# A third PSUM bank in both score tiles of a planned attention kernel, lent to side work when it is free

## The chip, the cores and the metric

One core of a Trainium2 chip. The metric is the device time of one execution in microseconds (us). TensorE is PE in the profile (PEld: its weight loads), VectorE is DVE, ScalarE is ACT, GpSimd is POOL. The profiled span runs from the first to the last instruction; it is 1.8 to 2.0 us shorter than the device time of the same execution. The profiled execution need not be the median one: the old kernel's has a span of 925.2 us, the median is 929.9 us.

## The reference

Two attention blocks over the same tokens (2048 tokens, width 640, 32 heads of 20), mixed by a gate per token:

```python
g = sigmoid((x * gate_w).sum(-1, keepdims=True))
a = softmax_attention(x, A_wqkv) @ A_wo        # full 2048 x 2048 scores, 32 heads
b = dilated_window_attention(x, B_wqkv) @ B_wo # 8 keys at distance 0, 2, ..., 14
return g * a + (1 - g) * b
```

Block A costs 2048 "units", each a 128 x 512 piece of scores that must be made by TensorE, passed through an exponential, and multiplied with V (PV). A head group is 64 units (four heads, 512 queries); there are 32.

## The kernel before

The Python program *plans*: it keeps an estimated clock per engine, lets generators (projections, block B, output) ask for TensorE time, VectorE time or a PSUM bank, and appends each instruction to its engine's list when the estimate says that it fits. The hardware then runs those lists with semaphores. So a small edit can move thousands of instructions.

Main loop, in short: take two or three units, make their scores (`qk`), take their exp on ScalarE, run PV of tiles two or more back, fill the rest of TensorE's time with side work (projections, block B, output), then with throw-away "filler" matmuls (`filler`). Some units skip ScalarE: each is a "ride", which VectorE copies out of PSUM; four rides make a "quad", from which VectorE makes five "slices" of exponentials.

```python
TSZ = (3, 2)                                   # banks of the two score tiles
score = [ps(512 * TSZ[0], "score0"), ps(512 * TSZ[1], "score1")]
obank = ps(512, "obank")                       # PV result
side = [ps(512, "side0"), ps(512, "side1")]    # for all other matmuls
NE = 6                                         # exp buffers, 1536 or 1024 wide
ebuf = [sb([P, 512 * TSZ[i % 2]], BF16, "ebuf%d" % i) for i in range(NE)]
NS = 3                                         # buffers of exp slices made by VectorE
...
def qk(s):                                     # scores of tile s; [cut]
    t = T("pe", 0.215, fn, reads=..., writes=[("score", s % 2)], mode="row")
    if rides[s]:                               # a "ride": unit 3 goes to VectorE, not ScalarE
        run_dve(t.end + LAT["pe"] - 0.35)
        T("dve", 0.69, lambda e: e.tensor_scalar(uD[...], o, UOFF, 0.0, op0=ALU.add, op1=ALU.max),
          reads=[("score", s % 2)], writes=[("uD", d % 2, i)])
def exp(s):
    n = len(tiles[s])
    exps[s] = T("act", actc(512 * n), lambda e: e.activation(
        ebuf[s % NE][:, 0:512 * n], score[s % 2][:, 0:512 * n], ACTF.Exp, scale=LN2 / STEP), ...)
...
def gen_d(d):                                  # five slices per ridden quad: int16 bit tricks for exp
    T("dve", 0.11 + 0.1334 * n, lambda e: e.tensor_scalar(eD[:, sl % NS, 0:512 * n].bitcast(I16),
      uD[d % 2][:, 0:512 * n], 0.25, SHIFTS[k], op0=ALU.mult, op1=ALU.add), ...)
def gen_bweights():                            # rearranges block B's weights, once
    for m in range(3):
        for c in range(CN):
            T("pool", 2.2, lambda e, o=o, i=i: e.tensor_copy(o, i), ...)   # 15 copies, 128 x 640
...
while pvg < NG:                                # main loop
        while s >= NE and pvq and tile_of[pvq[0]][0] <= s - NE:
            hold = 0                           # exp buffer of tile s not yet free:
            _, last = pv_slot(s, True)         # PV is forced, before the scores of tile s
            ...
        us = next_tile()
        ...
        qk(s); exp(s)
        if s >= hold and (s % 2 == 0 or ...):
            got, last = pv_slot(...)           # the regular place of PV
        spend(exps[s - 1].end + SLACK[len(us) - 2])   # side work and filler
```

Of the kernel before, what the change touches and what calls it, by code (L numbers as in the profile page):

```python
# [14 lines left out]
P = 128  # L15
# [3 lines left out]
DH = 20  # L19
# [226 lines left out]
def _build(ctx, nc, A_x, A_wqkv, A_wo, B_wqkv, B_wo, gate_w, out):  # L246
# [6 lines left out]

    TSZ = (3, 2)
    score = [ps(512 * TSZ[0], "score0"), ps(512 * TSZ[1], "score1")]
    obank = ps(512, "obank")
    side = [ps(512, "side0"), ps(512, "side1")]


    NE = 6  # L260
    NV0 = 2
# [7 lines left out]
    qT = [sb([P, 512], BF16, "qT%d" % i) for i in range(2)]  # L269
    ebuf = [sb([P, 512 * TSZ[i % 2]], BF16, "ebuf%d" % i) for i in range(NE)]  # L270
    NSLOT = 16
# [150 lines left out]

    bank_free = [0.0, 0.0]
    bank_used = [False, False]

# [6 lines left out]
    def release(b, t):  # L432
        bank_used[b] = False
        bank_free[b] = t.end + LAT[t.stream]

# [81 lines left out]
    def gen_v(half):  # L517
        for kb in range(NV0 if half == 0 else 0, KBN):
            b = yield from bank()
            mms = [(side[b][:, 0:320], xT[:, c, kb * P:(kb + 1) * P],  # L520
                    kvw[:, WV_OFF + c * D + half * 320:WV_OFF + c * D + half * 320 + 320]) for c in range(CN)]
            yield from mm_group(b, mms, ["WvA"] + XT(kb // 4), mmc(320))
            yield ("dve",)
            o = _ap(vA, (kb * NQ + 4 * half) * 4 * DV + 1, [[DV, 16], [1, DH]])
            i = _ap(side[b], 0, [[DH, 16], [1, DH]])
            t = T("dve", dvc(320), lambda e, o=o, i=i: e.tensor_copy(o, i), reads=[("side", b), "vAones"],
                  writes=[("vA", kb, half)])
            release(b, t)
            done[("v", kb, half)] = True
# [81 lines left out]
    def gen_bproj(u):  # L611
# [4 lines left out]
        for m in range(3):  # L616
# [5 lines left out]
            for f0 in range(0, CN, 2):  # L622
# [10 lines left out]
                o = tt[:, f0:f0 + n, off:off + TOK]  # L633
                i = _ap(side[b], 0, [[TOK, n], [1, TOK]])
                t = TB(dvc(n * TOK), lambda e, o=o, i=i: e.tensor_copy(o, i), reads=[("side", b)], writes=[key])
# [5 lines left out]
    def gen_b(u):  # L641
# [28 lines left out]
        if u == 0:  # L670
            yield ("pe", 0.06, 0.0)
            ob = _ap(side[b], 0, [[TOK, 2], [1, 16]])
            T("pe", 0.06, lambda e, ob=ob: e.matmul(ob, ident[:, :], maskB[:, :, :], start=False, stop=True, skip_group_check=True),
              reads=["ident", "maskB"], accum=[("side", b)])
# [57 lines left out]
        for f0 in range(0, CN, 2):  # L732
# [6 lines left out]
            o = oB[:, f0:f0 + n, hu * TOK:(hu + 1) * TOK]  # L739
            i0 = _ap(side[b], 0, [[TOK, n], [1, TOK]])  # L740
            i1 = _ap(rB, 0, [[0, n], [1, TOK]])
# [118 lines left out]
    def step(ent, limit, force):  # L860
# [10 lines left out]
        elif req[0] == "act":  # L871
            if not force and req[1] > sch.avail["act"]:
                return False
        elif req[0] == "bank":
            best = None
            for b in range(2):
                if not bank_used[b] and (best is None or bank_free[b] < bank_free[best]):
                    best = b
            if best is None or (not force and bank_free[best] > now):
                return False  # L880
            bank_used[best] = True
            send = best
        try:
# [6 lines left out]
        return moved  # L890

    def run_side(limit, force=False):
        while True:
            for ent in list(gens):
                if ent in gens and step(ent, limit, force):
# [22 lines left out]
    def turn(tcc, c0, c1, s_):  # L918
# [10 lines left out]

        T("pe", 0.065 * 4 * (c1 - c0), fn, reads=[("xs", tcc), "ident"], writes=[("score", s_)])  # L930

# [5 lines left out]
    def x_out(tcc):  # L937
        cols = slice(tcc * 512, (tcc + 1) * 512)
        T("act", actc(1536), lambda e: e.activation(  # L939
            xT[:, 0:3, cols], _ap(score[0], 0, [[512, 3], [1, 512]]), ACTF.Copy), reads=[("score", 0)], writes=[("xT", tcc, 0)])  # L940
        T("dve", dvc(1024), lambda e: e.tensor_copy(xT[:, 3:5, cols], _ap(score[1], 0, [[512, 2], [1, 512]])),
# [48 lines left out]
    for i in range(4):  # L990
# [9 lines left out]
    k_out(0)  # L1000
    T("pe", 1.07, proj5(side[1][:, :], lambda c: WqP[:, c, :], None, 0), reads=WQ + XT(0), writes=[("side", 1)])
    k_first(1)
# [6 lines left out]
    T("dve", dvc(512), lambda e: e.tensor_scalar(  # L1009
        qabs[:, :].bitcast(U16), side[1][:, :].bitcast(U16)[:, 1:1024:2], 0x7FFF, None, op0=ALU.bitwise_and),  # L1010
      reads=[("side", 1)], writes=["qabs"])
    k_max(2)
# [7 lines left out]
      reads=[("kmx", 0), "KMmask"], writes=[("KM", 0)])  # L1020
    T("pe", 0.215, lambda e: e.matmul(side[1][:, :], KM[0][:, :], qabs[:, :], start=False, stop=True, skip_group_check=True),
      reads=[("KM", 0), "qabs"], accum=[("side", 1)])
    t = k_out(3)
    obank_first = t.end + LAT["act"]
    v_out(0, 2, 1)
    t = T("dve", dvc(512), lambda e: e.tensor_scalar(qT[0][:, :], side[1][:, :], OCT, offs[:, 0:1], op0=ALU.mult, op1=ALU.add),
          reads=[("side", 1), "offs"], writes=[("qT", 0)])
    bank_free[0] = bank_free[1] = t.end + LAT["dve"]
    done[("k", 0)] = done[("q", 0)] = True
# [37 lines left out]

    DWAIT = 0.6

    def wanted(js):  # L1070
# [72 lines left out]
    def next_tile():  # L1143
        s = len(tiles)
        n = TSZ[s % 2]
        us = []
        ride = None
        while len(us) < n and cur["g"] < NG:
# [8 lines left out]
            if lo == 4 * hi:  # L1157
                cur["g"] += 1
                continue
            if n == 3 and len(us) == 2 and not ride:  # L1160
                ride = wanted([j for j in range(4) if all(uu % 4 != j for uu in us)])
# [9 lines left out]
        return us  # L1171

    def qk(s):
        us = tiles[s]
        sc = score[s % 2]
        lst = [(uu // 64, uu % 64 // 4, uu % 4, sc[:, i * 512:(i + 1) * 512]) for i, uu in enumerate(us)]
        if rides[s]:
            d, i, j = rides[s]
            o = sc[:, 1024:1536]
            lst.append((*dquads[d], j, o))  # L1180

# [9 lines left out]
        for g, kb, j, _ in lst:  # L1191
            rd.add(("kT", GROUPS[g][1], kb // 4))
            rd.add(("qT", g % 2))
        t = T("pe", 0.215, fn, reads=sorted(rd, key=str), writes=[("score", s % 2)], mode="row")
        if rides[s]:

            run_dve(t.end + LAT["pe"] - 0.35)
            T("dve", 0.69, lambda e: e.tensor_scalar(  # L1198
                uD[d % 2][:, 512 * i:512 * (i + 1)], o, UOFF, 0.0, op0=ALU.add, op1=ALU.max),
              reads=[("score", s % 2)], writes=[("uD", d % 2, i)])  # L1200
            if d == len(dquads) - 1 and not dopen:
                d_close()

    def exp(s):
        n = len(tiles[s])
        exps[s] = T("act", actc(512 * n), lambda e: e.activation(  # L1206
            ebuf[s % NE][:, 0:512 * n], score[s % 2][:, 0:512 * n], ACTF.Exp, scale=LN2 / STEP),
          reads=[("score", s % 2)], writes=[("ebuf", s % NE)])

# [36 lines left out]
    def filler(limit):  # L1246

        if sch.load(2.3) >= FILL:
            return False
        best = [b for b in range(2) if not bank_used[b] and bank_free[b] <= sch.avail["pe"]]  # L1250
        if best:
# [93 lines left out]
    while pvg < NG:  # L1345
# [44 lines left out]
        if acting:  # L1390
            lim = (exps[s - 1].end if s >= 1 else sch.avail["act"]) + SLACK[len(us) - 2]
            spend(lim)
# [36 lines left out]
```

## Time and profile before

929.9 us (median; one run took 1967 us and is left out).

Groups of instructions with different shapes kept apart (count, then busy us and mean ns, then the engine's idle time before them): the two widths of exp, and the two groups of filler.

```profile
L1206 ACT ACTIVATE ebuf<-score 128x1024 bf16<-128x1024 f32 x585 | 578.3, 1033 | 11.5 <-PE score L1186 8.5
L1206 ACT ACTIVATE ebuf<-score 128x1536 bf16<-128x1536 f32 x234 | 342.6, 1464 | 1.4 <-PE score L1186 0.7 <-ACT ebuf L1206 0.2
L1260 PE MATMUL obank<-xT,zero 128*32 128x512 bf16 x1240 | 100.4, 382 | 0.0
L1260 PE MATMUL side<-xT,ident 128*32 128x512 bf16 x452 | 37.2, 382 | 0.0
```

Durations overlap: neighbouring exps start 0.904 us (narrow) or 1.331 us (wide) apart when nothing delays them. I call 585 x 0.904 + 234 x 1.331 = 840.3 us the *floor* of the exps, and what start-to-start times exceed it by their *lateness*. (An exp's own duration is 1.03 us, so one that waits for its scores already loses 0.13 us before the profile shows idle time.) The span is then: 21.0 us head, 840.3 floor, 47.3 lateness, 16.4 tail (0.1 us is the last exp's own overlap).

The tail, as the timeline of ScalarE shows it (start, duration; in brackets idle time and who ended it):

```profile
907.27 1.45 ACT L1206 ACTIVATE ebuf<-score 128x1536 bf16<-128x1536 f32 x1
920.65 1.08 ACT L811 ACTIVATE stage<-side 128x512 bf16<-128x512 f32 x2 [11.93 <-PE side L792]
```

After the last exp TensorE still has 11 us of output projection to do.

### The profile page before, as it was taken

What the parts mean: (1) busy time and instruction counts of PE and PEld (TensorE: products, weight loads), DVE (VectorE), ACT (ScalarE), POOL (GpSimd) and SP (SyncE); (2) the same over time, 40 slices, a digit from 0 to 9 for tenths busy, and PEclk for the clock granted to TensorE, in tenths of its full rate; (3) what the DMA queues carried; (4) which work ended last, traced back from release to release, by engine and by line L of the source; (5) the groups of instructions that cost most, each with busy time, mean ns of one, the idle gap of its engine ahead of it and who ended that gap; (6) DMA issues with size and microseconds to landing.
All of it is one profiled execution on the core that took longest, in us unless ns stands there. A gap on an engine that the chain in (4) does not pass through costs nothing.

```text
span 925.2 us, 31488 instructions
## 1 busy us (share of the span) xinstructions
PE 908.8 (98%) x13998; PEld 322.6 (35%) x13998; DVE 676.6 (73%) x1173; ACT 889.1 (96%) x854; POOL 25.5 (3%) x23
## 2 busy tenths in 40 slices
PE   8999999998999999999999999999999999999997
PEld 4433332222333333333433343343343333433333
DVE  6667767887778768866886687577775956886862
ACT  6999999998999999999999999999999999999993
POOL 1000000008000000000000000000000000000000
PEclk9999999999999999999999999999999999999999
DMA  6121000030000010001100100110000001100000
GB/s 194 27 54 10 7 2 6 6 113 7 6 7 2 7 21 7 7 2 14 14 7 7 21 7 2 14 14 7 6 7 16 7 6 15 14 7 1 3 2 30
DMA packets 89027, 16.27 MB, mean 18 GB/s; under 512 B 81596, under 2 KB 88252, under 8 KB 88892
## 3 DMA queue, kind: packets, MB, share of 16 engines
q1 hardware_dynamic: 88892, 14.27, 9.5%
q8 instruction: 110, 1.80, 0.8%
q14 instruction: 25, 0.20, 0.1%
HBM read 11.63 MB, written 2.62 MB: 15 GB/s over the span
## 4 chain that ended last, share of the span: by engine, by line
PE 77%; ACT 18%; issue 3%; DVE 1%; DMA 0%; DVEq 0%; ACTq 0%
PE side L449 26%; PE score L1186 24%; ACT ebuf L1206 18%; PE obank L1239 16%; PE obank L1260 6%; PE side L1260 2%; PE side L662 1%; PE side L717 1%; DMA oTn<-in_A_x_dram 0%; PE score L926 0%; DVE eD L587 0%; ACT xT L939 0%; PE obank L947 0%; PE side L947 0%; DVE oTt L570 0%
## 5 line engine op out<-in xcount | busy, mean ns | idle before, releaser
L1206 ACT ACTIVATE ebuf<-score 128x1024 bf16<-128x1024 f32 (+1 forms) x819 | 871.4, 1156 | 13.0 <-PE score L1186 9.3
L1186 PE MATMUL score<-qT,kT 32*128 32x512 bf16 x2048 | 334.6, 384 | 7.2 <-ACT ebuf L1206 3.4
L1198 DVE TENSOR_SCALAR uD<-score 128x512 uint16<-128x512 f32 x176 | 121.1, 688 | 107.1 <-PE score L1186 105.0
L1186 PEld LDWEIGHTS score<-qT,kT 32*128 32x128 bf16 x2048 | 79.8, 91 | 284.4 <-issue 131.5
L1239 PE MATMUL obank<-ebuf,vA 128*21 128x512 bf16 x1872 | 175.3, 385 | 2.0 <-DVE eD L587 1.4
L587 DVE TENSOR_SCALAR eD<-uD 128x2048 int16<-128x2048 uint16 x220 | 146.0, 692 | 9.9 <-PE obank L1239 8.9
L449 PE MATMUL side<-xT,kvw 128*32 128x256 bf16 (+1 forms) x2960 | 141.1, 294 | 0.0
L1260 PE MATMUL obank<-xT,zero 128*32 128x512 bf16 x1240 | 100.4, 382 | 0.0
L449 PEld LDWEIGHTS side<-xT,kvw 128*32 128x32 bf16 x2960 | 69.4, 96 | 45.5 <-issue 22.4
L1239 PEld LDWEIGHTS obank<-ebuf,vA 128*21 128x21 bf16 x1872 | 41.3, 89 | 110.6 <-issue 93.1
L1239 PE MATMUL obank<-eD,vA 128*21 128x512 bf16 x880 | 71.2, 379 | 0.0
L729 DVE TENSOR_TENSOR stage<-vB,repB 128x1280 bf16<-128x1280 bf16 x64 | 50.4, 820 | 0.9
L449 PE MATMUL side<-stage,ident 128*32 128x512 bf16 (+1 forms) x768 | 50.2, 346 | 0.0
L652 DVE TENSOR_TENSOR stage<-qB,kB 128x1280 bf16<-128x1280 bf16 x64 | 49.7, 817 | 0.1
L449 PE MATMUL side<-woA_r,oTn 128*32 128x512 bf16 (+1 forms) x992 | 49.3, 300 | 0.0
L449 PE MATMUL side<-xT,WqP 128*32 128x512 bf16 x620 | 48.4, 382 | 0.0
L1260 PEld LDWEIGHTS obank<-xT,zero 128*32 128x32 bf16 x1240 | 28.3, 95 | 33.6 <-issue 21.7
L1260 PE MATMUL side<-xT,ident 128*32 128x512 bf16 x452 | 37.2, 382 | 0.0
L449 PE MATMUL side<-woBp,oB 128*32 128x512 bf16 (+1 forms) x640 | 33.7, 301 | 0.5 <-issue 0.5
L449 PE MATMUL side<-kvw,xT 128*32 128x320 bf16 x600 | 30.6, 300 | 0.2 <-DVE qT L512 0.2
L472 DVE TENSOR_SCALAR kT<-side,onesrow 128x512 bf16<-128x512 f32 x28 | 21.0, 749 | 12.3 <-PE side L449 12.2
L742 DVE SCALAR_TENSOR_TENSOR oB<-side,rB 128x512 bf16<-128x512 f32 (+1 forms) x24 | 14.4, 598 | 19.8 <-PE side L449 19.7
(122 smaller groups left out, 575.5 us busy)
## 6 DMA issues: line engine op xcount, KB each, us to landing
WqP<-in_A_wqkv_dram SPq DMA_DIRECT2D x150, 20.0 KB, 2.3
stage<-in_B_wqkv_dram SPq DMA_DIRECT2D x1, 2400.0 KB, 9.1
out_dram<-outsb SPq DMA_DIRECT2D x12, 160.0 KB, 1.9
oTn<-in_A_x_dram SPq DMA_DIRECT2D x2, 640.0 KB, 5.2
kvw<-in_A_wqkv_dram SPq DMA_DIRECT2D x1, 800.0 KB, 8.8
stage<-in_A_wqkv_dram SPq DMA_DIRECT2D x1, 800.0 KB, 9.9
woA_r<-in_A_wo_dram SPq DMA_DIRECT2D x4, 200.0 KB
woBp<-in_B_wo_dram SPq DMA_DIRECT2D x5, 160.0 KB
```

What stands on the lines that cost most here:

```text
L449: ins = e.matmul(o[32 * j:32 * j + 32, :], l[:, 32 * j:32 * j + 32], r, start=(first and i == 0), stop=(last and i == n - 1), skip_group_c ...
L472: t = T("dve", dvc(512), lambda e, b=b, tcc=tcc: e.tensor_scalar(kT[:, q, tcc * 512:(tcc + 1) * 512], side[b][:, :], onesrow[:, 0:1], None ...
L587: T("dve", 0.11 + 0.1334 * n, lambda e, k=k, sl=sl: e.tensor_scalar(eD[:, sl % NS, 0:512 * n].bitcast(I16), uD[d % 2][:, 0:512 * n], 0.25, ...
L652: TB(dvc(CN * TOK, 2), lambda e, w=w, ks=ks: e.tensor_tensor(prodB(w), qB[:, :, :], ks, ALU.mult), reads=["qB", "kB"], writes=[("prod", w) ...
L662: ins = e.matmul(side[b][32 * w4:32 * w4 + 32, half * TOK:(half + 1) * TOK], Sel, pr, start=(half == 0 and f == 0), stop=(half == 1 and f ...
L729: TB(dvc(CN * TOK, 2), lambda e, w=w, vs=vs, rr=rr: e.tensor_tensor(prodB(w), vs, rr, ALU.mult), reads=["vB", ("repB", w4 % 2)], writes=[( ...
L742: t = TB(dvc(n * TOK), lambda e, o=o, i0=i0, i1=i1: e.scalar_tensor_tensor(o, i0, -0.5, i1, op0=ALU.mult, op1=ALU.mult), reads=[("side", b ...
L1186: ins = e.matmul(o, kT[32 * j:32 * j + 32, q, kb * P:(kb + 1) * P], qT[g % 2][32 * j:32 * j + 32, :], start=True, stop=True)
L1198: T("dve", 0.69, lambda e: e.tensor_scalar(uD[d % 2][:, 512 * i:512 * (i + 1)], o, UOFF, 0.0, op0=ALU.add, op1=ALU.max), reads=[("score", ...
L1206: exps[s] = T("act", actc(512 * n), lambda e: e.activation(ebuf[s % NE][:, 0:512 * n], score[s % 2][:, 0:512 * n], ACTF.Exp, scale=LN2 / S ...
L1239: ins = e.matmul(obank[32 * j:32 * j + DV, :], vA[:, kb, GROUPS[g][1], j, :], src, start=(kb == 0), stop=(last and k >= len(lst) - 4), ski ...
L1260: ins = e.matmul(o[32 * j:32 * j + 32, :], w[:, 32 * j:32 * j + 32], xT[:, 0, 0:512], start=bool(best), stop=bool(best), skip_group_check= ...
```

## The change

Both score tiles get three banks. The third bank of each is a shared resource: for a wide exp, for a ride to VectorE, or for side work. One side bank stays fixed. At most two of the three are held by side work at once. To fit, the exp buffers become five of 1536 (the same bytes as six alternating ones).

```diff
-    TSZ = (3, 2)
-    score = [ps(512 * TSZ[0], "score0"), ps(512 * TSZ[1], "score1")]
+    score = [ps(1536, "score0"), ps(1536, "score1")]
-    side = [ps(512, "side0"), ps(512, "side1")]
-    NE = 6
+    sbank = ps(512, "side0")
+    BANKS = [(sbank, 0), (score[0], 1024), (score[1], 1024)]
+    side = [t_[:, o_:o_ + 512] for t_, o_ in BANKS]
+    NE = 5
-    ebuf = [sb([P, 512 * TSZ[i % 2]], BF16, "ebuf%d" % i) for i in range(NE)]
+    ebuf = [sb([P, 1536], BF16, "ebuf%d" % i) for i in range(NE)]
@@ bank request: a lent bank only if no matmul is ready, never the last of the three
+            if best is None or sum(bank_used) == NB - 1 or (not force and bank_free[best] > now):
+                return False
+            if best and not force and (ent[0] > XPRIO or any(...)):
+                return False
@@ side work that holds a lent bank goes first (order(), BOOST, XBOOST)
@@ next_tile
-        n = TSZ[s % 2]
+        free = not bank_used[x] and bank_free[x] <= now + XTOL and not crowded(x)
+        n = 3 if free else 2
@@ qk: the third bank is waited for only where it is used; RFILL = 0.0
-            run_dve(t.end + LAT["pe"] - 0.35)
+            run_dve(t.end + LAT["pe"] - RFILL)
... (names of banks in the other generators, and in the head and the tail)
```

More of the change, by code (lines that the diff above doesn't have):

```diff
@@ L251, in _build @@
     T = sch.task
-    TSZ = (3, 2)
-    score = [ps(512 * TSZ[0], "score0"), ps(512 * TSZ[1], "score1")]
+    score = [ps(1536, "score0"), ps(1536, "score1")]
     obank = ps(512, "obank")
-    side = [ps(512, "side0"), ps(512, "side1")]
-    NE = 6
+    sbank = ps(512, "side0")
+    BANKS = [(sbank, 0), (score[0], 1024), (score[1], 1024)]
+    NB = len(BANKS)
+    side = [t_[:, o_:o_ + 512] for t_, o_ in BANKS]
+    sap = lambda b, off, dims: _ap(BANKS[b][0], BANKS[b][1] + off, dims)
+    NE = 5
     NV0 = 2
@@ L420, in w_pad @@
         return lambda e: e.tensor_copy(o, i)
-    bank_free = [0.0, 0.0]
-    bank_used = [False, False]
+    bank_free = [0.0] * NB
+    bank_used = [False] * NB
+    bank_own = [None] * NB
     def bank():
@@ L433, in release @@
         bank_used[b] = False
+        bank_own[b] = None
         bank_free[b] = t.end + LAT[t.stream]
@@ L524, in gen_v @@
             o = _ap(vA, (kb * NQ + 4 * half) * 4 * DV + 1, [[DV, 16], [1, DH]])
-            i = _ap(side[b], 0, [[DH, 16], [1, DH]])
+            i = sap(b, 0, [[DH, 16], [1, DH]])
             t = T("dve", dvc(320), lambda e, o=o, i=i: e.tensor_copy(o, i), reads=[("side", b), "vAones"],
@@ L633, in gen_bproj @@
                 o = tt[:, f0:f0 + n, off:off + TOK]
-                i = _ap(side[b], 0, [[TOK, n], [1, TOK]])
+                i = sap(b, 0, [[TOK, n], [1, TOK]])
                 t = TB(dvc(n * TOK), lambda e, o=o, i=i: e.tensor_copy(o, i), reads=[("side", b)], writes=[key])
@@ L671, in gen_b @@
             yield ("pe", 0.06, 0.0)
-            ob = _ap(side[b], 0, [[TOK, 2], [1, 16]])
+            ob = sap(b, 0, [[TOK, 2], [1, 16]])
             T("pe", 0.06, lambda e, ob=ob: e.matmul(ob, ident[:, :], maskB[:, :, :], start=False, stop=True, skip_group_check=True),
@@ L739, in gen_b @@
             o = oB[:, f0:f0 + n, hu * TOK:(hu + 1) * TOK]
-            i0 = _ap(side[b], 0, [[TOK, n], [1, TOK]])
+            i0 = sap(b, 0, [[TOK, n], [1, TOK]])
             i1 = _ap(rB, 0, [[0, n], [1, TOK]])
@@ L875, in step @@
             best = None
-            for b in range(2):
-                if not bank_used[b] and (best is None or bank_free[b] < bank_free[best]):
+            for b in range(NB):
+                if not bank_used[b] and (best is None or max(bank_free[b], now) < max(bank_free[best], now)):
                     best = b
-            if best is None or (not force and bank_free[best] > now):
+            if best is None or sum(bank_used) == NB - 1 or (not force and bank_free[best] > now):
+                return False
+            if best and not force and (ent[0] > XPRIO or any(o_[3][0] == "pe" and o_[3][2] <= now + 0.3 for o_ in gens)):
                 return False
             bank_used[best] = True
+            bank_own[best] = ent
             send = best
@@ L890, in step, with order @@
         return moved
+    BOOST = 4.5
+    XBOOST = 4.0
+    XPRIO = 9.0
+    def order():
+        return sorted(gens, key=lambda e: e[0] - (BOOST if e[3][0] == "dve" and any(e is o_ for o_ in bank_own) else
+                                                   XBOOST if any(e is o_ for o_ in bank_own[1:]) else 0.0))
     def run_side(limit, force=False):
         while True:
-            for ent in list(gens):
+            for ent in order():
                 if ent in gens and step(ent, limit, force):
@@ L928, in fn @@
             return ins
-        T("pe", 0.065 * 4 * (c1 - c0), fn, reads=[("xs", tcc), "ident"], writes=[("score", s_)])
+        T("pe", 0.065 * 4 * (c1 - c0), fn, reads=[("xs", tcc), "ident"],
+          writes=[("score", s_)] + ([("side", 1)] if c1 - c0 == 3 else []))
     def turned(tcc):
@@ L939, in x_out @@
         T("act", actc(1536), lambda e: e.activation(
-            xT[:, 0:3, cols], _ap(score[0], 0, [[512, 3], [1, 512]]), ACTF.Copy), reads=[("score", 0)], writes=[("xT", tcc, 0)])
+            xT[:, 0:3, cols], _ap(score[0], 0, [[512, 3], [1, 512]]), ACTF.Copy), reads=[("score", 0), ("side", 1)], writes=[("xT", tcc, 0)])
         T("dve", dvc(1024), lambda e: e.tensor_copy(xT[:, 3:5, cols], _ap(score[1], 0, [[512, 2], [1, 512]])),
@@ L1000, in _build @@
     k_out(0)
-    T("pe", 1.07, proj5(side[1][:, :], lambda c: WqP[:, c, :], None, 0), reads=WQ + XT(0), writes=[("side", 1)])
+    T("pe", 1.07, proj5(side[2][:, :], lambda c: WqP[:, c, :], None, 0), reads=WQ + XT(0), writes=[("side", 2)])
     k_first(1)
@@ L1009, in _build @@
     T("dve", dvc(512), lambda e: e.tensor_scalar(
-        qabs[:, :].bitcast(U16), side[1][:, :].bitcast(U16)[:, 1:1024:2], 0x7FFF, None, op0=ALU.bitwise_and),
-      reads=[("side", 1)], writes=["qabs"])
+        qabs[:, :].bitcast(U16), side[2][:, :].bitcast(U16)[:, 1:1024:2], 0x7FFF, None, op0=ALU.bitwise_and),
+      reads=[("side", 2)], writes=["qabs"])
     k_max(2)
@@ L1020, in _build @@
       reads=[("kmx", 0), "KMmask"], writes=[("KM", 0)])
-    T("pe", 0.215, lambda e: e.matmul(side[1][:, :], KM[0][:, :], qabs[:, :], start=False, stop=True, skip_group_check=True),
-      reads=[("KM", 0), "qabs"], accum=[("side", 1)])
+    T("pe", 0.215, lambda e: e.matmul(side[2][:, :], KM[0][:, :], qabs[:, :], start=False, stop=True, skip_group_check=True),
+      reads=[("KM", 0), "qabs"], accum=[("side", 2)])
     t = k_out(3)
@@ L1025, in _build @@
     v_out(0, 2, 1)
-    t = T("dve", dvc(512), lambda e: e.tensor_scalar(qT[0][:, :], side[1][:, :], OCT, offs[:, 0:1], op0=ALU.mult, op1=ALU.add),
-          reads=[("side", 1), "offs"], writes=[("qT", 0)])
-    bank_free[0] = bank_free[1] = t.end + LAT["dve"]
+    t = T("dve", dvc(512), lambda e: e.tensor_scalar(qT[0][:, :], side[2][:, :], OCT, offs[:, 0:1], op0=ALU.mult, op1=ALU.add),
+          reads=[("side", 2), "offs"], writes=[("qT", 0)])
+    bank_free[:] = [t.end + LAT["dve"]] * NB
     done[("k", 0)] = done[("q", 0)] = True
@@ L1068, in _build @@
     DWAIT = 0.6
+    XTOL = 0.2
+    RFILL = 0.0
     def wanted(js):
@@ L1144, in next_tile @@
         s = len(tiles)
-        n = TSZ[s % 2]
+        x = 1 + s % 2
+        now = max(sch.avail["pe"], exps[s - 2].end + LAT["act"] if s > 1 else 0.0)
+        free = not bank_used[x] and bank_free[x] <= now + XTOL and not crowded(x)
+        n = 3 if free else 2
         us = []
@@ L1159, in next_tile @@
                 continue
-            if n == 3 and len(us) == 2 and not ride:
+            if len(us) == 2 and not ride:
                 ride = wanted([j for j in range(4) if all(uu % 4 != j for uu in us)])
@@ L1171, in next_tile, with crowded @@
         return us
+    def crowded(x):
+        return sum(bank_used) == 1 and any(ent[3][0] == "bank" for ent in gens) and bank_free[x] <= min(
+            [bank_free[b] for b in range(NB) if not bank_used[b]])
     def qk(s):
         us = tiles[s]
+        x = 1 + s % 2
         sc = score[s % 2]
@@ L1178, in qk @@
             d, i, j = rides[s]
-            o = sc[:, 1024:1536]
-            lst.append((*dquads[d], j, o))
+            lst.append((*dquads[d], j, side[x]))
         def fn(e):
@@ L1193, in qk @@
             rd.add(("qT", g % 2))
-        t = T("pe", 0.215, fn, reads=sorted(rd, key=str), writes=[("score", s % 2)], mode="row")
+        t = T("pe", 0.215, fn, reads=sorted(rd, key=str),
+              writes=[("score", s % 2)] + ([("side", x)] if len(lst) == 3 else []), mode="row")
         if rides[s]:
-            run_dve(t.end + LAT["pe"] - 0.35)
-            T("dve", 0.69, lambda e: e.tensor_scalar(
-                uD[d % 2][:, 512 * i:512 * (i + 1)], o, UOFF, 0.0, op0=ALU.add, op1=ALU.max),
-              reads=[("score", s % 2)], writes=[("uD", d % 2, i)])
+            run_dve(t.end + LAT["pe"] - RFILL)
+            t = T("dve", 0.69, lambda e: e.tensor_scalar(
+                uD[d % 2][:, 512 * i:512 * (i + 1)], side[x], UOFF, 0.0, op0=ALU.add, op1=ALU.max),
+              reads=[("side", x)], writes=[("uD", d % 2, i)])
+            bank_free[x] = t.end + LAT["dve"]
             if d == len(dquads) - 1 and not dopen:
@@ L1205, in exp @@
         n = len(tiles[s])
+        x = 1 + s % 2
         exps[s] = T("act", actc(512 * n), lambda e: e.activation(
             ebuf[s % NE][:, 0:512 * n], score[s % 2][:, 0:512 * n], ACTF.Exp, scale=LN2 / STEP),
-          reads=[("score", s % 2)], writes=[("ebuf", s % NE)])
+          reads=[("score", s % 2)] + ([("side", x)] if n == 3 else []), writes=[("ebuf", s % NE)])
+        if n == 3:
+            bank_free[x] = exps[s].end + LAT["act"]
     def pv(units, slices):
@@ L1249, in filler @@
             return False
-        best = [b for b in range(2) if not bank_used[b] and bank_free[b] <= sch.avail["pe"]]
+        best = [b for b in range(NB) if not bank_used[b] and bank_free[b] <= sch.avail["pe"]]
         if best:
@@ L1390, in _build @@
         if acting:
-            lim = (exps[s - 1].end if s >= 1 else sch.avail["act"]) + SLACK[len(us) - 2]
+            lim = (exps[s - 1].end if s >= 1 else sch.avail["act"]) + SLACK[max(0, len(us) - 2)]
             spend(lim)
```

## The prediction

> **What bounds it now.** ScalarE. The engine table gives it 889 of 925.2 us (96%). TensorE shows 98%, but the Trainium skill ("Trainium Kernel Development and Optimization", Performance Expectations) calls matmul busy time a bad metric, and this trace agrees: 1,692 matmuls, about 91 us at the plan's 0.215 us per four, are filler (groups of lines, L1260). The timeline splits the span: 21.0 us before the first exp; 819 exps until 908.7 us; a tail of 16.5 us, in which ScalarE idles 11.9 us while TensorE finishes the output projection's prefold (L449, until 920.0).
>
> Between exps, start-to-start times are at least 0.904 us (1024 wide) and 1.331 us (1536 wide). So 585 + 234 exps need 840 us of the 888; about 47 us are exps starting late, mostly on a tile whose third bank went to VectorE (mean 0.12 us late, 176 times) and after one (0.06 us). The idle column shows 13 us only, since a late exp first loses its overlap with the one before.
>
> **What the change does, counted in the instruction order.** Exps: 585 to 631 narrow, 234 to 198 wide. ScalarE: 631 x 0.904 + 198 x 1.331 = 834 against 840: **-6 us**. VectorE gets 16 rides (now 192) and 20 exp slices of 0.69 us, +25 us, to 76% busy: not binding. TensorE loses 352 filler matmuls and gains 64 PV matmuls.
>
> Still at most two side banks are held at once, but any two of three. Side work ends earlier: after the last score tile the old kernel's leftover side work runs from 908.8 to 920.0 us; the new one has 80 matmuls of 512 columns left. At the 0.24 us per four seen there, that is 5 us against 11; the last normalisation (2.7 us) is hidden as before. Tail: **-6 us**.
>
> The filler agrees: 19 us less, of which 6 is prefold moved forward and 3 PV; the rest fits a main stretch 6 us or more shorter.
>
> **What it costs.** Narrow exps following narrow ones rise from 352 to 495, and these are the late ones. With the old lateness by kind of pair (narrow-to-narrow without a ride put at 0.06 us, my estimate): +4 us. A wide tile now needs its third bank back from VectorE; the plan puts a 512-wide copy at 0.63 us, the trace has 0.69 to 0.75, so some score matmuls will wait: +2 us, estimate. Five exp buffers instead of six may make exps wait for PV at group ends: +1 us. Waits of TensorE for rides fall: -1 us.
>
> **Sum.** -6 -6 +4 +2 +1 -1 = -6 us; the filler count argues for -12. I take -10: **920 us**, range 911 to 928. Faster by over 2%: 0.09; within: 0.87; slower: 0.04.
>
> **What would show it.** Exp busy time about 865 us instead of 871; first exp still at 21 us; last exp ending at 903 to 906 us; from there to the end 10 to 12 us instead of 16.5; ScalarE's idle before its last copies about 6 us instead of 11.9. New waits of score matmuls for VectorE evacuations (kT, qT, vA, repB, kB) under 8 us. Filler near 72 us.
>
> **What would make it wrong.** If VectorE lags the plan in dense stretches, waits for the third bank pass to ScalarE, and the exp stretch gets longer. If five exp buffers stall ScalarE at each of 32 group ends, up to 10 us come back. If narrow exps were late through TensorE's load rather than through rides, lateness may move 10 us either way.

## More of the kernel before

From the page of the profiled execution: busy time by engine, and the span in 40 slices of 23 us (a digit is the busy share in tenths).

```profile
span 925.2 us, 31488 instructions
PE 908.8 (98%) x13998; PEld 322.6 (35%) x13998; DVE 676.6 (73%) x1173; ACT 889.1 (96%) x854; POOL 25.5 (3%) x23
DVE  6667767887778768866886687577775956886862
ACT  6999999998999999999999999999999999999993
POOL 1000000008000000000000000000000000000000
```

ScalarE is full from the first to the last slice but one. TensorE's 98% holds filler.

ScalarE's waits for scores (total us, times, longest us):

```profile
ACT ebuf L1206 <- PE score L1186: 9.3, 27, 1.8
```

## The result and the profile after

926.6 us against 929.9 us in the first rounds, ratio 0.998 (95% interval 0.996 to 1.000); in five more rounds 927.6 against 928.0 us, ratio 0.999 (0.998 to 1.001). Ratios here are from runs of the same rounds; they are not quite the ratio of the medians (0.996 in the first result). The old kernel's fast runs spread from 925.5 to 930.1 us in the five rounds, so a difference of 0 to 3 us is all that can be said: no change clear of noise. This spread goes with TensorE's mean granted clock: the old kernel's executions at 0.999 took 925.5 to 926.9 us, those at 0.996 took 929.8 to 930.1 us. The changed kernel had 0.994 to 0.996 in every execution. The old kernel's profile is of an execution at 0.999.

```profile
span 924.7 us, 31431 instructions
PE 905.5 (98%) x13935; PEld 322.1 (35%) x13938; DVE 697.6 (75%) x1209; ACT 881.4 (95%) x864; POOL 27.2 (3%) x23
DVE  6567778888888787988777877787786778678552
ACT  6999999996999999999999999999999999999996
POOL 1000000027000000000000000000000000000000
```

ScalarE is 8 us less busy, and its last slice is fuller. But in GpSimd's slice it falls to 6. Shapes apart, the answer to the groups above:

```profile
L1239 ACT ACTIVATE ebuf<-score 128x1024 bf16<-128x1024 f32 x631 | 607.9, 1037 | 23.1 <-PE score L1216 20.0 <-ACT ebuf L1239 0.2
L1239 ACT ACTIVATE ebuf<-score 128x1536 bf16<-128x1536 f32 x198 | 282.4, 1469 | 3.9 <-PE score L1216 3.2
L1295 PE MATMUL side<-xT,ident 128*32 128x512 bf16 x772 | 57.3, 382 | 0.0
L1295 PE MATMUL obank<-xT,zero 128*32 128x512 bf16 x568 | 46.3, 384 | 0.0
L1295 PE MATMUL score<-xT,ident 128*32 128x512 bf16 x228 | 19.9, 385 | 0.0
```

The exps fell as forecast (631 narrow, 198 wide, floor 834.0 us). The idle time before them doubled. Filler now has a third row: 228 matmuls write into a lent bank, whose name is `score`. ScalarE's tail, and its waits:

```profile
920.30 0.60 ACT L818 ACTIVATE stage<-score 128x512 bf16<-128x512 f32 x1 [5.35 <-PE score L799]
```

```profile
ACT ebuf L1239 <- PE score L1216: 23.2, 49, 3.0
```

Sum, in us, head to tail:

| | head | floor | lateness | tail | span |
|---|---|---|---|---|---|
| before | 21.0 | 840.3 | 47.3 | 16.4 | 925.2 |
| after | 21.0 | 834.0 | 59.9 | 9.8 | 924.7 |
| difference | 0 | -6.3 | +12.6 | -6.6 | -0.4 |

Two gains of 6 us each came as forecast, and 12.6 us of new lateness took them. Of that, 6.3 us lie between 200 and 250 us alone (lateness there 4.8 us before, 11.1 us after). In that stretch the changed kernel shows (timeline; first VectorE, then TensorE):

```profile
203.96 5.31 DVE L594 TENSOR_SCALAR eD<-uD 128x2048 int16<-128x2048 uint16 x3
215.15 6.22 DVE L594 TENSOR_SCALAR eD<-uD 128x2048 int16<-128x2048 uint16 x4
...
209.32 0.40 PE L1274 MATMUL obank<-ebuf,vA 128*21 128x512 bf16 x4 [2.78 <-DVE eD L594]
223.34 0.40 PE L456 MATMUL score<-xT,WqP 128*32 128x512 bf16 x4 [2.88 <-DVE uD L1229]
```

Three slices took 5.3 us where 1.9 is usual (the same three in a row, at 205.4 us of the old kernel). TensorE stood still for 2.78 and for 2.88 us: once in front of PV that needs a slice, once in front of side work that was given a lent bank and waited for VectorE to read the ride out of it, behind four slow slices. And next to it GpSimd, in the old and in the changed kernel:

```profile
206.84 22.60 POOL L601 COPY kvw<-stage 128x640 bf16<-128x640 bf16 x15 [198.28 <-PE side L449]
```

```profile
202.50 24.26 POOL L608 COPY kvw<-stage 128x640 bf16<-128x640 bf16 x15 [193.96 <-PE score L456]
```

After each of these two standstills TensorE's granted clock fell (to 0.5 for 3.4 us each time), which it did not in the old kernel's profiled execution (windows; busy us of PE, PEld, DVE, ACT, POOL, then the granted clock, DMA share and GB/s). Old, then changed kernel:

```profile
210.00:215.00 5.00, 4.96 (x61) 1.23 (x57) 3.10 (x4) 5.00 (x6) 4.82 (x4) 1.00 0.00 2
225.00:230.00 5.00, 4.92 (x97) 2.40 (x101) 4.58 (x9) 4.42 (x5) 4.32 (x3) 1.00 0.02 3
```

```profile
210.00:215.00 5.00, 4.85 (x51) 0.88 (x43) 3.63 (x6) 3.36 (x4) 4.82 (x4) 0.66 0.00 0
225.00:230.00 5.00, 5.00 (x54) 1.26 (x51) 3.54 (x8) 3.14 (x4) 1.69 (x2) 0.73 0.26 16
```

### The profile page after: what moved, and what is told of

The parts are those of the page before. It is cut to its first block, busy times and chain, and to the rows that moved or that the text cites. A ratio compares the mean times of both kernels' runs of the same rounds, so it can differ in the third digit from the quotient of the medians.

```text
span 924.7 us, 31431 instructions
## 1 busy us (share of the span) xinstructions
PE 905.5 (98%) x13935; PEld 322.1 (35%) x13938; DVE 697.6 (75%) x1209; ACT 881.4 (95%) x864; POOL 27.2 (3%) x23
## 4 chain that ended last, share of the span: by engine, by line
PE 82%; ACT 12%; DVE 2%; issue 2%; DVEq 0%; ACTq 0%
PE score L1216 25%; PE obank L1274 18%; PE score L456 16%; PE side L456 12%; ACT ebuf L1239 12%; PE side L1295 3%; PE obank L1295 3%; DVE eD L594 1%; PE score L1295 1%; PE score L669 1%; PE side L669 0%; PE obank L366 0%; PE score L945 0%; PE side L724 0%; PE score L724 0%
## 5 line engine op out<-in xcount | busy, mean ns | idle before, releaser
L1239 ACT ACTIVATE ebuf<-score 128x1024 bf16<-128x1024 f32 (+1 forms) x829 | 863.5, 1140 | 27.0 <-PE score L1216 23.2
L456 PE MATMUL score<-xT,kvw 128*32 128x256 bf16 (+1 forms) x1780 | 87.2, 299 | 0.8 <-ACT ebuf L1239 0.6
L456 PE MATMUL side<-xT,kvw 128*32 128x256 bf16 (+1 forms) x1180 | 54.6, 289 | 0.2 <-DVE qT L519 0.2
L456 PEld LDWEIGHTS score<-xT,kvw 128*32 128x32 bf16 x1780 | 40.6, 95 | 30.4 <-issue 19.0
L1295 PE MATMUL obank<-xT,zero 128*32 128x512 bf16 x568 | 46.3, 384 | 0.0
L456 PEld LDWEIGHTS side<-xT,kvw 128*32 128x32 bf16 x1180 | 27.6, 96 | 17.3 <-issue 10.6
L1274 PEld LDWEIGHTS obank<-eD,vA 128*21 128x21 bf16 x960 | 23.8, 92 | 16.6 <-issue 1.9
L608 POOL COPY kvw<-stage 128x640 bf16<-128x640 bf16 x15 | 23.4, 1560 | 194.8 <-PE score L456 194.0
L456 PE MATMUL score<-xT,WqP 128*32 128x512 bf16 x300 | 25.0, 396 | 2.9 <-DVE uD L1229 2.9
L456 PE MATMUL side<-stage,ident 128*32 128x512 bf16 (+1 forms) x352 | 26.8, 372 | 0.0
L456 PE MATMUL score<-woA_r,oTn 128*32 128x128 bf16 (+1 forms) x568 | 26.7, 290 | 0.0
```

The costliest lines, as they stand in the source:

```text
L456: ins = e.matmul(o[32 * j:32 * j + 32, :], l[:, 32 * j:32 * j + 32], r, start=(first and i == 0), stop=(last and i == n - 1), skip_group_c ...
L608: T("pool", 2.2, lambda e, o=o, i=i: e.tensor_copy(o, i), reads=["stage"], writes=[("WkP", qq) for qq in range(NQ)] + ["WvA", ("wBp", m)])
L1239: exps[s] = T("act", actc(512 * n), lambda e: e.activation(ebuf[s % NE][:, 0:512 * n], score[s % 2][:, 0:512 * n], ACTF.Exp, scale=LN2 / S ...
L1274: ins = e.matmul(obank[32 * j:32 * j + DV, :], vA[:, kb, GROUPS[g][1], j, :], src, start=(kb == 0), stop=(last and k >= len(lst) - 4), ski ...
L1295: ins = e.matmul(o[32 * j:32 * j + 32, :], w[:, 32 * j:32 * j + 32], xT[:, 0, 0:512], start=bool(best), stop=bool(best), skip_group_check= ...
```

## The experiments

**Theory A**: the 15 weight copies of GpSimd hold VectorE's slices off. The Trainium skill states such a lock ("SBUF — State Buffer", Who interferes with whom): VectorE in its two-port modes, or with two inputs in SBUF against a GpSimd instruction that reads SBUF, and GpSimd share a port pair, and whoever has it keeps it for a whole instruction. **Rival B**: the loss is spread over the span, by narrow exps and waits for lent banks. **Theory C** came later, from what stands in front of late scores: five exp buffers are too few. **Rival D**: that is the narrow tiles' doing.

Each kernel below ran beside the old one on the same chip, on four chips (medians of the old kernel there: 928.0, 928.2, 928.1 and 927.3 us). The table's first two rows are the first result. Lateness is taken from each profiled execution. "Behind PV" is the lateness of exps whose score matmuls directly follow PV on TensorE; "behind side" of those that follow side work. The other kinds (behind filler, or with another ScalarE instruction between) stay at 8 to 13 us but for the two `qkf` runs.

| run | median us | ratio to old | floor | lateness | behind PV | behind side | tail |
|---|---|---|---|---|---|---|---|
| old | 929.9 | 1 | 840.3 | 47.3 | 6.2 | 28.8 | 16.4 |
| changed | 926.6 | 0.998 | 834.0 | 59.9 | 31.5 | 19.8 | 9.8 |
| nopool_before | 923.9 | 0.996 | 840.3 | 44.4 | 5.3 | 28.6 | 16.3 |
| nopool_after | 918.2 | 0.990 | 834.0 | 51.3 | 27.7 | 15.3 | 9.8 |
| noride_after | 930.8 | 1.003 | 839.4 | 58.3 | 33.0 | 17.0 | 9.8 |
| split_before | 924.2 | 0.996 | 840.3 | 44.6 | 5.4 | 28.7 | 16.3 |
| split_after | 919.7 | 0.991 | 834.0 | 53.3 | 27.9 | 17.0 | 9.8 |
| ne5_before | 936.0 | 1.007 | 836.9 | 56.4 | 17.3 | 28.7 | 16.7 |
| qkfirst_after | 936.7 | 1.009 | 834.6 | 68.5 | 8.3 | 35.1 | 10.0 |
| qkf_split_after | 930.4 | 1.002 | 834.6 | 62.3 | 6.2 | 33.8 | 10.0 |
| ne6ns2_split | 910.0 | 0.980 | 837.4 | 39.7 | 10.6 | 20.2 | 10.1 |
| pvevery_split | 916.8 | 0.988 | 836.7 | 47.8 | 16.7 | 22.4 | 9.4 |
| rfill_split | 923.0 | 0.995 | 837.6 | 52.7 | 27.1 | 16.9 | 9.6 |
| ne5ns2_split | 926.4 | 1.000 | 839.0 | 54.3 | 28.5 | 17.0 | 10.0 |
| split2_before | 932.1 | 1.004 | 838.6 | 43.8 | 5.4 | 29.3 | 24.1 |

### The gain, timed again (after_again)

> The changed kernel itself, timed against the old one in five rounds, to size the gain: both theories below start from it. The first result gave medians of 926.6 against 929.9 us but a ratio of 0.9979 that still included 1, and profiled spans of 924.7 against 925.2 us. I expect a ratio between 0.995 and 0.999.

No edit. 927.6 against 928.0 us, ratio 0.9994 (0.998 to 1.001). The gain is smaller than the first medians let it seem.

### GpSimd's copies taken away (nopool_before, nopool_after)

```diff
+    o, i = _ap(kvw, (m * CN + c) * D, [[1, 4]]), _ap(stage, c * 3 * D + m * D, [[1, 4]])
     T("pool", 2.2, lambda e, o=o, i=i: e.tensor_copy(o, i), reads=["stage"], ...)
```

(A memset of a part of `kvw` on GpSimd at the start keeps memory defined. Block B then has wrong weights: the output is wrong, as measured. The planned order of TensorE, VectorE and ScalarE is the same to the instruction.)

> Old kernel; the 15 copies of weights on GpSimd (206.8 to 229.4 us in its trace) are cut to 4 elements each; instruction order of every other engine unchanged; output wrong on purpose. Theory A (the copies slow VectorE's fast SBUF-to-SBUF instructions, and score matmuls behind them come late): the lateness of exps between 200 and 250 us falls from 4.8 us to about 2.5, so the kernel gains 2 to 3 us. Rival B (the late exps of that stretch come from the plan alone): gain under 1 us.

> Changed kernel with the same cut; order of every other engine unchanged; output wrong on purpose. Theory A: exp slices of VectorE return from 1.8 to 0.69 us between 202 and 227 us, lateness there falls from 11.1 to about 3 us, and the kernel gains 7 to 8 us: three times as much as the old one gains, about 918 to 919 us. Rival B (the gain was lost to narrow exps and third-bank waits all over the span): it gains no more than the old one does, under 3 us.

Changed kernel: 918.2 us, ratio 0.9895; old kernel: 923.9 us, ratio 0.9956. On the kernels' medians of the same rounds that is 9.4 us for the changed and 4.2 us for the old one. Theory A forecast 7 to 8 and 2 to 3; rival B forecast equal gains and is out as the explanation of the whole. Lateness at 200 to 250 us fell from 11.1 to 3.2 and from 4.8 to 2.1 us. Part of the gains goes with the clock: without the copies no execution of either kernel was under 0.999, and against only those executions of the unedited old kernel that had 0.999, the old kernel gains 1.6 to 3.0 us. The slices of VectorE between 202 and 230 us (count, then min/median/max ns) in the old kernel, the changed one, and the changed one without copies:

```profile
L587 DVE TENSOR_SCALAR eD<-uD x9: 683/689/1839, 202.8 to 229.7; 128x2048 int16<-128x2048 uint16 x9
```

```profile
L594 DVE TENSOR_SCALAR eD<-uD x9: 681/1821/1849, 204.0 to 219.6; 128x2048 int16<-128x2048 uint16 x9
```

```profile
L595 DVE TENSOR_SCALAR eD<-uD x16: 682/686/695, 203.8 to 229.7; 128x2048 int16<-128x2048 uint16 x16
```

The plan of the change happens to put its slices where GpSimd copies; the old one puts most of its own elsewhere. Two things agree with the skill's rule: instructions that read PSUM (the rides, 0.69 us) and reductions kept their time, and in the old kernel a 128 x 16 `tensor_tensor` with both inputs in SBUF took 1.04 us beside the copies instead of 0.18.

Without copies the two kernels differ by 5.7 us (923.9 - 918.2): that is what the change is worth with this cost out of the way. The tail gives 6.5 of it. The exp stretch gives nothing: the floor's -6.3 is met by +6.9 of lateness. Its make-up is the surprise: behind PV +22.4 us, behind side work -13.3 us.

### No new rides while GpSimd copies (noride_after)

```diff
+            if now < sch.avail["pool"] and now > 100.0:
+                return None
     T("pool", 1.7, ...)   # planned at 2.2 before
```

> Changed kernel; no new quad is opened for VectorE while GpSimd copies weights (planned at 1.7 us a copy); right output. The order has 180 rides instead of 192, so the floor of all exps rises from 834.0 to 839.4 us. Theory A: lateness falls by about 7 us and pays for the 5.4 us: time within 2 us of the changed kernel. Rival B: lateness unchanged, 5 us slower.

930.8 us, 3.3 us slower than the changed kernel in the same rounds. Lateness fell by 1.6 us only: the slices of quads opened before the copies still ran beside them (five of six took 1.80 to 1.85 us), and 12 rides were lost. The outcome is nearer to what was expected of B than of A; but the edit missed its aim, so it decides nothing between them.

### Smaller copies (split_after, split_before)

```diff
-                T("pool", 2.2, lambda e, o=o, i=i: e.tensor_copy(o, i), ...)
+                def fn(e, m=m, c=c):
+                    for f in range(CN):                     # five copies of 128 x 128
+                        ins = e.tensor_copy(<fifth f of o>, <fifth f of i>)
+                    return ins
+                T("pool", 2.2, fn, ...)
```

> Changed kernel; each of the 15 GpSimd weight copies is split into 5 of a fifth of the size; planned order of all other engines unchanged; right output. Theory A, refined (a VectorE slice waits for the one GpSimd copy under way, so shorter copies mean shorter waits): slices next to the copies take 0.7 to 1.2 us instead of 1.8, lateness of exps at 200 to 250 us falls from 11 to about 4 us, and the kernel gains 5 to 8 us, to about 920 us. If GpSimd holds VectorE off for as long as any copy is queued: no gain, or a loss, since the copies take longer in all.

> Old kernel with the weight copies split in five as well; planned order of all other engines unchanged; right output. Theory A: it gains what it gained without copies, 3 to 5 us, so about 924 us, and the pair with split copies (919.7 against about 924) shows the change's gain without the lock: 4 to 6 us. If the split helped the changed kernel for another reason: no gain here.

919.7 us, right output, 8 us under the changed kernel's 927.6 (of the other rounds; ratios to the old kernel 0.991 against 0.999). Lateness at 200 to 250 us fell to 4.6 us. GpSimd needs 37 us in place of 24, yet a slice now takes at most 0.92 us, as if it waited for one short copy:

```profile
L594 DVE TENSOR_SCALAR eD<-uD x14: 757/897/922, 203.8 to 229.5; 128x2048 int16<-128x2048 uint16 x14
```

The old kernel gains 3.9 us by it (924.2 us). So the lock, with the falls of the clock that come with it, took about 4 us of the old kernel's median and 8 to 9 of the changed one's; with it mended the change is worth 4.5 us (924.2 - 919.7, runs of two calls).

### One part of the change alone: five exp buffers (ne5_before)

```diff
-    NE = 6
-    ebuf = [sb([P, 512 * TSZ[i % 2]], BF16, "ebuf%d" % i) for i in range(NE)]
+    NE = 5
+    ebuf = [sb([P, 1536], BF16, "ebuf%d" % i) for i in range(NE)]
```

> Old kernel with one part of the change alone: five exp buffers of 1536 instead of six of alternating size; right output. The order puts PV matmuls straight before a score tile 100 times instead of 59; rides go from 176 to 184, so the floor of all exps falls from 840.3 to 836.9 us. Theory C (five buffers force PV in front of score matmuls, and exps come late): lateness behind such PV rises from 5.9 us to 11 or more, so the time is 1 to 5 us longer in spite of the lower floor. Rival D (PV stands in front of score tiles in the changed kernel because its tiles are narrow): lateness behind PV stays under 8 us, and the time falls by about 3 us with the floor.

936.0 us, 7.8 us slower than the old kernel, though its floor fell by 3.4 us. Lateness behind PV rose from 6.2 to 17.3 us, behind side work it stayed at 28.7. That is theory C, at a larger cost than it forecast. Not all of the 7.8 us comes from the buffers: lateness at 200 to 250 us was 8.1 us, which is again the lock, and four of the six executions had a lower clock (0.993 to 0.994, 935.7 to 936.6 us) than the profiled one (0.998, 932.9 us). ScalarE's waits for scores, 9.3 us in the old kernel, here:

```profile
ACT ebuf L1206 <- PE score L1186: 16.4, 42, 2.2
```

What it looks like, in the changed kernel without copies at the end of a head group (timeline of TensorE, VectorE's left out; then ScalarE's exp):

```profile
356.44 0.62 PE L1297 MATMUL obank<-xT,zero 128*32 128x512 bf16 x8
...
357.26 0.61 PE L1276 MATMUL obank<-ebuf,vA 128*21 128x512 bf16 x8
357.70 0.82 PE L1276 MATMUL obank<-eD,vA 128*21 128x512 bf16 x12
358.45 0.61 PE L1218 MATMUL score<-qT,kT 32*128 32x512 bf16 x5
...
358.95 1.02 ACT L1241 ACTIVATE ebuf<-score 128x1024 bf16<-128x1024 f32 x1 [0.83 <-PE score L1218]
```

An exp buffer must come free, so 20 PV matmuls stand in front of the scores that ScalarE waits for.

### PV after the scores instead of before them (qkfirst_after, qkf_split_after)

```diff
-            while s >= NE and pvq and tile_of[pvq[0]][0] <= s - NE: ...   # before qk(s)
             qk(s)
+            while s >= NE and pvq and tile_of[pvq[0]][0] <= s - NE: ...   # the same loop
             exp(s)
```

> Changed kernel; the PV matmuls that must free an exp buffer are issued after the score matmuls of the tile, before its exp, instead of before the score matmuls; right output. PV straight before a score tile falls from 152 to 86 times; floor 834.6 instead of 834.0. Theory C: lateness behind PV falls from 31 to about 18 us and the kernel gains 6 to 12 us. Rival: the exp then waits for the PV itself, so the lateness only moves and the gain is under 2 us.

> Both remedies together, right output: if A and C are separate costs their gains add, 12 to 18 us under the changed kernel, 910 to 915 us; if they are the same microseconds, no more than the better of the two.

936.7 us and, with split copies, 930.4 us: slower than without, and far from the 910 to 915 us of the sum. Lateness behind PV did fall (31.5 to 8.3 us), but the exp needs its buffer, and now waits for the PV itself. The wait changed its name, as the rival said; that the kernel would lose 9 us neither side said. From the profile of the first:

```profile
ACT ebuf L1239 <- PE obank L1274: 23.0, 47, 2.3
ACT ebuf L1239 <- PE score L1216: 9.3, 20, 1.9
```

So the shortage of buffers has to go, not the order. (The copies cost 6 us here too: 936.7 - 930.4. Part of it goes with the clock, which beside the copies was 0.5 for 10.2 us of the profiled execution.)

### A sixth buffer, or earlier PV (ne6ns2_split, pvevery_split)

```diff
 # ne6ns2_split (on split_after)          # pvevery_split (on split_after)
-    NE = 5                               -        if s >= hold and (s % 2 == 0 or not acting or ...
-    NS = 3                               +        if s >= hold and (s % 2 == 0 or len(pvq) > 8 or ...
+    NE = 6
+    NS = 2
```

> Changed kernel with split copies, six exp buffers of 1536 instead of five; the room comes from two buffers of exp slices instead of three; right output. The order puts PV straight before a score tile 102 times instead of 152; floor of all exps 837.4 instead of 834.0 us, 184 rides instead of 192. Theory C: lateness behind PV falls from 28 to 18 us or less, so the time is 3 to 8 us under the 919.7 us. Rival D (narrow tiles as such): lateness unchanged, and the time rises by 3 us or more with the floor.

> Changed kernel with split copies and five exp buffers; a PV slot is also given after odd tiles when more than eight units are waiting, so buffers come free before they are wanted; right output. PV straight before a score tile 84 times instead of 152, floor 836.7 instead of 834.0 us. Theory C: lateness behind PV falls from 28 to 15 us or less, and the kernel gains 3 to 9 us. Rival: the score matmuls come late behind other work instead, so total lateness stays above 50 us and the time rises by 3 us.

With six buffers 910.0 us, ratio 0.980 (0.979 to 0.982): faster than both kernels, right output, and the best found; whether by 2% over the old one is open, as the interval spans it. The gain over 919.7 us is 9.7 us, more than the 3 to 8 forecast. Lateness behind PV fell from 27.9 to 10.6 us. Rival D forecast 923 us and no less lateness; its tiles are about as narrow (623 narrow of 829). With PV given earlier 916.8 us, lateness behind PV 16.7 (forecast: 15 or less, and a gain of 3 to 9 us; it was 2.9). ScalarE's waits for scores, in the kernel with split copies and in the one with six buffers:

```profile
ACT ebuf L1245 <- PE score L1222: 16.8, 43, 1.5
```

```profile
ACT ebuf L1245 <- PE score L1222: 5.5, 13, 1.4
```

### The ride's fill undone (rfill_split)

```diff
-    RFILL = 0.0
+    RFILL = 0.35
```

> Changed kernel with split copies and one part of the change undone: VectorE's queue ahead of a ride is again filled only to 0.35 us before the ride's scores are ready; right output. Floor 837.6 instead of 834.0 us. If this part is what lowered the lateness behind side work (from 28.8 us in the old kernel to about 17), that lateness rises by 5 us or more and the time by 8 us or more; if the lent banks did it, it stays within 3 us and the time rises by about 3 us with the floor.

923.0 us: 3.4 us slower, with the floor (+3.6). Lateness behind side work stayed (16.9 against 17.0 us), so this part of the change did not bring it down from 28.8; the lent banks or the new order of side work did. Which of these two, I did not test.

### Six exp buffers or two slice buffers (ne5ns2_split, split2_before)

```diff
 # ne5ns2_split: on split_after           # split2_before: on split_before
-    NS = 3                               -    NS = 3
+    NS = 2                               +    NS = 2
```

> Changed kernel with split copies, five exp buffers and two slice buffers: the six-buffer version's means of making room, without its sixth buffer; right output. Floor 839.0 us, PV straight before a score tile 168 times. Theory C (the sixth exp buffer made the gain): lateness behind PV stays at 25 us or more and the time at 920 us or more. Rival E (fewer slice buffers did it, by making PV slots shorter): lateness behind PV falls to 15 us or less, time about 912 us.

> Old kernel with split copies and two slice buffers instead of three (its six exp buffers stay); right output. Floor 838.6 instead of 840.3 us. Theory C: within 3 us of the 924.2 us with three slice buffers, so against it the six-buffer version of the changed kernel shows the change's gain without the shortage. Rival E: it falls by 6 us or more.

With two slice buffers and five exp buffers 926.4 us, lateness behind PV 28.5 us: the sixth exp buffer, with the plan that it allows, is worth 16 us (926.4 - 910.0, runs of two calls). ScalarE's waits for scores, against the 5.5 us with six buffers:

```profile
ACT ebuf L1245 <- PE score L1222: 18.0, 47, 0.9
```

Two slice buffers gave nothing: in the old kernel the time rose to 932.1 us. That was 5 us outside what I expected of C; its exp stretch ended 2 us earlier, but its plan left 24 us of tail. So the tail too is an outcome of the plan, and the change's shorter one is shown for these plans, not as a property of lent banks. The same caution holds for every size above but those of the `nopool` and `split` runs, which keep the planned order: each other variant is a new plan, and here a new plan alone moved the time by 8 us.

## Why the prediction was wrong

The time lay in the range and "within 2%" was right, but I forecast -10 us and got between 0 and -3.

- **ScalarE's floor, -6 us: right.** 834.0 us as counted, exp busy time 863.5 us (forecast about 865).
- **Tail, -6 us: right.** 16.4 to 9.8 us (forecast 10 to 12); ScalarE's idle before the last copies 5.35 us (about 6).
- **Lateness, +6 us in sum: the step that failed.** It measured +12.6 us, so the last exp ended at 915.0 us, not at 903 to 906. Half of the rise (6.3 us) lies beside GpSimd's copies: the lock, which the prediction left out. The evidence lay in the old trace: a slice of 1.84 us beside the copies, and ScalarE's 8 in GpSimd's slice. The skill's page on SBUF names the lock; I had read VectorE's busy share and taken each slice at 0.69 us wherever the plan puts it. The prediction's own list of what would make it wrong names both roads of the loss, VectorE behind its plan and stalls at group ends with five exp buffers, but its sum had only +2 us (waits for third banks) and +1 us on them.
- **"Five exp buffers ... +1 us": far too small.** Lateness behind PV rose by 25 us (by 22 without copies). It was masked by a gain for which the sum had at most the 1 us of shorter waits for rides: lateness behind side work fell by 9 us (13 without copies). The net outside GpSimd's stretch, +6.3 us, matched my sum by cancellation, not by insight.
- **"TensorE loses 352 filler matmuls ... the filler count argues for -12": a miscount.** I added the rows that write `obank` and `side` and overlooked the 228 that write a lent bank under the name `score`. The true loss is 1692 - 1568 = 124 matmuls, 7 us at the plan's 0.215 us per four, which leaves nothing for a shorter main stretch; filler was 84 us by that price, not 72. Without this step the forecast would have been its own sum, -6 us, and that is what the pairs without or with small copies show: -5.7 and -4.5 us.
- **Waits of scores for third banks: small, as forecast.** The large waits at the lent bank were behind slices that the lock held up.

So the expected gain went into two new waits: about 5 us to the lock (9.4 - 4.2), and the floor's 6 us, net of what the shorter lateness behind side work gave, to scores queued behind PV for want of an exp buffer.

## What to carry to other kernels

When a plan moves VectorE's fast SBUF-to-SBUF instructions, look at what GpSimd does at that moment; here each slice beside a long GpSimd copy took 1.1 us more, and cutting the copies into short ones mended most of it without touching the plan. When a buffer is paid for with another, cost the one that is given up by its own experiment: here five in place of six ate what was gained elsewhere, and a sixth, paid for with a slice buffer, took the kernel with short copies from 919.7 to 910.0 us. Count instructions by what they do, not by the tile they write, when a change renames tiles.

## What the Trainium skill lacked or had wrong

- "SBUF — State Buffer", Who interferes with whom: right about the lock. It does not say how a profile shows it: not as idle time but as a longer instruction (slices of 1.82 us in place of 0.69; GpSimd's own copies 1.56 us on average in place of the old kernel's 1.45), so busy shares hide it.
- The same page gives no remedy by size. Copies cut in five (75 of 0.53 us on average) brought the median slice to 0.90 us and the kernel 8 us down.
- "TensorE: Matmul & The Clock Gate", Why this matters for your kernels, advises against idle gaps over about 3 us. Here that length did not decide: the clock fell to 0.5 for 3.4 us after recorded gaps of 2.78 and 2.88 us in the changed kernel and of 2.38 us in `ne5_before`, did not fall after one of 2.78 us in `noride_after`, and fell in `ne5ns2_split` (at 643.5 us) where no recorded gap was over 1.5 us.
- "ScalarE: Activation LUTs", What ACT_TABLE_LOAD costs, puts the overlap of back-to-back ACTIVATEs at about 93 ns. Here, for exps that read PSUM, it was 0.13 us (mean duration less the least start to start: 1.033 - 0.904 and 1.464 - 1.331), and a late exp lost it before any idle time showed.
